# The finished fp16 rows reach x1 through 32x32 block transposes on VectorE and four plain transfers per pair of units, in place of two DMA transposes

## Chip, cores and metric

One core of a Trainium2 chip. The metric is the device time of one execution in microseconds; three runs of the kernel before are given with their median. A profile of one further execution shows what each engine did.

## What is computed

Four batches of 12,800 tokens with 128 channels. 49 agents per batch gather the values (softmax over the keys), and hand them out again to the queries (softmax over the agents). On the result x stand a gated causal convolution of five taps and an output projection:

```python
a2k = sm(agents, k)                 # 49 x 12800
agent_v = a2k @ v                   # 49 x 128
x = sm(q, agents) @ agent_v         # 12800 x 128
gate = sigmoid(sum_k conv_w[k] * x shifted by 4 - k)
out = (gate * (x @ w_val)) @ w_out
```

## The kernel before

x itself is never formed. agent_v, the conv weights and w_val are folded per batch into one set of matrices (`fold_weights`), so gate and value are matmuls of these with the query softmax weights. To keep precision with fp16 matmuls, each weight w stands as a high part and a low part in fp16. 49 high, 49 low and a second copy of 49 high make 147 rows; 128 of them stand in the tile `x1` (one row per partition, tokens along the free side), the 19 left over are put five times, once per tap shift, into the tile `x2` (95 rows).

The work runs in units of 1280 tokens, 10 units per batch (40 in all, g = 0 to 39); two units make a pair that shares one `x1` tile of 2560 tokens (ring of 4) and one `x2` tile (ring of 3). For each unit:

- `key_scores` and `agent_values`: scores of the keys (8 matmuls into the PSUM tile `sc`), copied to `ks`; later exp, VectorE's 32x32 transposes into `eT`, and 10 groups of matmuls into `av`.
- `queries`: scores into `sc`, VectorE transposes them to token-major `sT`; maximum, subtraction (POOL), exp (ACT), sum (VectorE), scaling (POOL) make the weights w in `qw`; then w is split into `pt`, 128 fp16 columns per token: ACT copies the high part, POOL writes the second copy (`again`) and the low part.
- `transposes`: brings `pt` to the row layout of `x1`. Units 0 to 3 go through TensorE and PSUM (`on_pe`). Units 4 to 39 go by one DMA transpose each (L845). `shifts` then sends the 19 rows into `x2` by two transfers per pair (L894), and `halo` copies four columns for the next pair.

Then chunks of 512 tokens, 25 per batch: `gates` (five matmuls of `x1`, L932, one of `x2`, L936, then tanh on ACT), `values` (L959, L963, then h = (th + 1) * val on VectorE, L972, and its split into `hh` on ACT and `hl` on POOL), `project` (L1004 to L1006, copied out by ACT and stored). The PSUM tiles gate, val, out and av exist once, `sc` twice.

The order: a long string lists PE's steps (k, v, q, t, g, a, o with batch and unit, or chunk). `Plan` records every instruction group with an estimated duration, its needs and its engine; PE's groups stand exactly in the order of the string, while the other engines and the DMA queue (all issued from SP, in order) are ordered by a list scheduler from those estimates. A transfer issued from SP that waits holds up those behind it. Loads go round a ring of 11 slots `ld`.

Of the kernel before, what the change touches and what calls it, by code (L numbers as in the profile page):

```python
# [10 lines left out]
F16 = mybir.dt.float16  # L11
# [6 lines left out]
P = 128  # L18
# [23 lines left out]
NPT = 4  # L42
# [148 lines left out]
def tile_agent_attention_gated_conv(  # L191
# [42 lines left out]
    pts = ring(NPT, [P, NBLK, P], F16, "pt")  # L234
# [198 lines left out]
    def key_max(b):  # L433
# [16 lines left out]
        def spread():  # L450
            nc.vector.tensor_reduce(
                out=mrow, in_=p1[0:2, 0:P].rearrange("j (g a) -> j a g", g=G),
                axis=AX.X, op=ALU.max,
            )
            nc.vector.tensor_copy(
                out=mrep, in_=mrow.unsqueeze(1).to_broadcast([2, G, BLK])
            )

        add("dve", 0.5, spread, [at1], ["mrep"])
# [61 lines left out]
    gs = const.tile([P, TAPS, A], F32, name="gs")  # L521
    rs = const.tile([P, 2], F32, name="rs")
# [4 lines left out]
    def fold_weights(b):  # L527
# [58 lines left out]
        ghi = wst[:, 0:TAPS, 0:A]  # L586
        vhi = wst[:, TAPS, 0:A]

        def thirds(x, first, end):
            return x[..., first:end:3]  # L590

        def lows(low, full, hi, less):


            for out, first, end in zip(low, (2, 0, 1, LAST), (A, LAST, A, A)):
                less(out, thirds(full, first, end), thirds(hi, first, end))

        def rest(out, full, s, hi):
            dve.scalar_tensor_tensor(
                out=out, in0=full, scalar=rs[:, s : s + 1], in1=hi,  # L600
                op0=ALU.mult, op1=ALU.subtract,
            )

        def val_weights():
# [9 lines left out]
            dve.tensor_scalar_mul(vhi, pv[:, 0:A], rs[:, 1:2])  # L614
            low = (
                wst[:, TAPS, 2 * A : 2 * A + THIRDS], wst[:, TAPS, 2 * A + THIRDS :],
                x2v[:, HALO, 0:THIRDS], x2v[:, HALO, THIRDS:],
            )
            lows(low, pv[:, 0:A], vhi, lambda out, full, hi: rest(out, full, 1, hi))

        gate_lows = (
            wst[:, 0:TAPS, 2 * A : 2 * A + THIRDS], wst[:, 0:TAPS, 2 * A + THIRDS :],
            x2g[:, :, 0:THIRDS], x2g[:, :, THIRDS:],
        )

        def gate_weights():
            dve.tensor_scalar_mul(ghi, gw, rs[:, 0:1])
# [6 lines left out]
        def gate_rest_pool():  # L634
# [10 lines left out]
        if b == 0:  # L645
            add("pool", 0.47, gate_scaled, ["gw", "rsg"], ["gs"])
            add("act", 0.4, lambda: nc.scalar.copy(out=ghi, in_=gs), ["gs"], [(*w_, "g")])
            add("pool", 1.27, gate_rest_pool, ["gs", (*w_, "g")], [(*w_, "r")])
        else:
            add("dve", 0.47, gate_weights, ["gw", "rsg"], [(*w_, "g")])  # L650
        add("dve", 1.58, val_weights, [at_v], [(*w_, "v"), "mxv"])
        add(
            "act", 0.4,
            lambda: nc.scalar.copy(out=wst[:, 0:TAPS, A : 2 * A], in_=ghi),
            [(*w_, "g")], [(*w_, "d")],
        )
# [10 lines left out]
        def transposes():  # L667
# [6 lines left out]
            "pe", 0.6, transposes, [(*w_, n) for n in "derv"] + [(*w_, "g")], [at_w],  # L674
# [68 lines left out]
    def queries(b, u):  # L743
# [7 lines left out]
        pt = pts[g % NPT]  # L751
# [27 lines left out]
        def weigh():  # L779
# [8 lines left out]
        p_ = ("pt", g % NPT)  # L788
        add(
            "act", 0.6, lambda: nc.scalar.copy(out=pt[:, :, A : 2 * A], in_=w),  # L790
            [("qw", g % NPT)], [(*p_, 0)],
        )

        def again():
            for o, end, first, last in ((2 * A, 2 * A + THIRDS, 2, A), (2 * A + THIRDS, P, 0, LAST)):
                nc.gpsimd.tensor_scalar(
                    out=pt[:, :, o:end], in0=w[:, :, first:last:3],
                    scalar1=1.0, scalar2=0.0, op0=ALU.mult, op1=ALU.add,
                )

        add("pool", 0.76, again, [("qw", g % NPT)], [(*p_, 2)])
        add(
            "pool", 1.09,
            lambda: nc.gpsimd.tensor_tensor(  # L804
                out=pt[:, :, 0:A], in0=w, in1=pt[:, :, A : 2 * A], op=ALU.subtract
            ),
            [("qw", g % NPT), (*p_, 0)], [(*p_, 1)],
        )
    def on_pe(b, u):
# [7 lines left out]
    def row_keys(s, halves):  # L817


        i = s % NX  # L820
        return [(x, i, h) for h in halves for x in ("x1", "x1b")] + [("x1h", i)] * (0 in halves)

    def halo(s):
# [4 lines left out]
        else:  # L828
# [3 lines left out]
            read = [(x, (s - 1) % NX, 1) for x in ("x1", "x1b")]  # L832
# [372 lines left out]
```

## Time and profile before

| what | value |
|---|---|
| median of three runs | 417.81 us (415.74, 417.81, 419.00) |
| the profiled execution | 415.52 us, of which span 413.4 us |
| granted TensorE clock, mean | 0.991 |
| busy PE / DVE / ACT / POOL | 395.0 / 256.0 / 297.8 / 282.1 us |
| DMA moved | 127.63 MB in 75,130 packets, 50,466 of them under 512 B |

The span runs from the first to the last instruction. Busy time of PE is modelled from the matmuls' starts, and pipelined matmuls overlap, so a busy PE is not by itself a PE at its peak. PEld is the weight load, DVE VectorE, ACT ScalarE, POOL GpSimd, SP the engine that issues the DMAs.

### The profile page before, as it was taken

Reading aid. Unit: us, or ns where it says so; the run is one execution under the profiler, and the core shown is the slowest. Engines: PE = TensorE matmul, PEld = TensorE weight load, DVE = VectorE, ACT = ScalarE, POOL = GpSimd, SP = SyncE. Lnnn points to the kernel's source line nnn. Section 1 sums busy time; section 2 is a strip of 40 time slices with the busy share of each in tenths; the row PEclk is TensorE's granted clock in tenths of the full one; section 3 lists DMA queues with packets and bytes.
Section 4 is the critical chain, followed back from the end, with each engine's and each line's share of the span. In section 5 each row is a group of like instructions: output and inputs, shape, how many; then the busy total and the mean of one; then the engine's idle time right before and its main releaser. Section 6 shows DMA issues by size and latency. Waiting matters only on the chain.

```text
span 413.4 us, 10115 instructions
## 1 busy us (share of the span) xinstructions
PE 395.0 (96%) x3905; PEld 197.1 (48%) x3905; DVE 256.0 (62%) x489; ACT 297.8 (72%) x519; POOL 282.1 (68%) x381
## 2 busy tenths in 40 slices
PE   4859999999999999999999999999999999999996
PEld 2348544445555434445446544445465544444443
DVE  3758688854835857566745687576664697643231
ACT  2564568597884777869885677689886676888875
POOL 1003679766878698656788775896578789998752
PEclk9969999999999999999999999999999999999999
DMA  8999999999999999999999999999999999999933
GB/s 323 420 416 411 366 360 357 284 358 252 350 320 267 336 269 317 337 306 330 346 356 296 298 347 311 340 303 342 310 348 313 261 302 291 223 251 232 216 144 138
DMA packets 75130, 127.63 MB, mean 309 GB/s; under 512 B 50466, under 2 KB 50850, under 8 KB 75084
## 3 DMA queue, kind: packets, MB, share of 16 engines
q1 hardware_dynamic: 74940, 126.87, 99.9%
q8 instruction: 30, 0.49, 0.5%
q10 hardware_dynamic: 144, 0.13, 0.2%
q14 instruction: 16, 0.13, 0.1%
HBM read 79.25 MB, written 26.21 MB: 255 GB/s over the span
## 4 chain that ended last, share of the span: by engine, by line
PE 85%; DMA 7%; ACT 3%; DVE 3%; POOL 1%; issue 1%; SPq 0%; DVEq 0%; ACTq 0%
PE gate L932 25%; PE sc L390 17%; PE av L494 11%; PE out L1004 5%; PE val L959 5%; PE gate L936 5%; PE val L963 5%; PE out L1005 5%; PE out L1006 5%; DMA ld<-kT 4%; DMA x<-x 2%; ACT e L485 1%; ACT th L945 1%; PE sc L859 1%; DVE h L972 0%
## 5 line engine op out<-in xcount | busy, mean ns | idle before, releaser
L985 POOL TENSOR_TENSOR hl<-h,hh 128x512 f16<-128x512 f32 x99 | 114.6, 1160 | 57.4 <-ACT hh L980 55.0
L932 PE MATMUL gate<-x,stat 128*128 128x512 f16 (+1 forms) x500 | 124.3, 378 | 0.6 <-ACT e L485 0.4
L972 DVE SCALAR_TENSOR_TENSOR h<-th,val 128x512 f32<-128x512 f32 x100 | 68.1, 681 | 81.6 <-PE out L1005 27.8
L390 PE MATMUL sc<-ld,ag_sb 128*32 128x320 f32 x1280 | 97.1, 442 | 7.5 <-DMA ld<-kT 6.3
L1025 ACT ACTIVATE ob<-out,oscale 128x512 f32<-128x512 f32 x98 | 67.2, 686 | 23.4 <-PE out L1006 23.3
L945 ACT ACTIVATE th<-gate,unscale 128x512 f32<-128x512 f32 x100 | 68.5, 685 | 21.3 <-PE gate L936 19.2
L932 PEld LDWEIGHTS <-stat 128*128 128x128 f16 x505 | 47.7, 97 | 60.6 <-issue 5.5
L980 ACT CAST hh<-h 128x512 f16<-128x512 f32 x99 | 60.7, 613 | 14.4 <-DVE h L972 13.8
L762 POOL TENSOR_TENSOR qw<-sT,qmx 128x490 f32<-128x490 f32 x40 | 40.5, 1018 | 43.8 <-DVE qmx L757 41.3
L390 PEld LDWEIGHTS sc<-ld,ag_sb 128*32 128x32 f32 x1280 | 37.9, 111 | 54.9 <-issue 17.4
L494 PE MATMUL av<-ld,eT 128*32 128x129 f32 (+1 forms) x1400 | 50.5, 277 | 2.2 <-DVE eT L400 2.2
L494 PEld LDWEIGHTS av<-ld,eT 128*32 128x32 f32 (+1 forms) x1400 | 45.6, 115 | 10.3 <-issue 3.4
L416 ACT COPY ks<-sc 128x640 f32<-128x640 f32 x40 | 27.6, 693 | 27.3 <-PE sc L390 25.1
L400 DVE STREAM_TRANSPOSE sT<-sc 128x640 f32<-128x640 f32 x40 | 33.5, 842 | 19.9 <-PE sc L390 19.1
L400 DVE STREAM_TRANSPOSE eT<-e 128x640 f32<-128x640 f32 x40 | 33.5, 839 | 19.1 <-ACT e L485 11.2
L804 POOL TENSOR_TENSOR pt<-qw,pt 128x490 f16<-128x490 f32 x40 | 43.9, 1104 | 1.9 <-ACT pt L790 1.8
L485 ACT ACTIVATE e<-ks,kbias 128x320 f32<-128x320 f32 x80 | 39.4, 554 | 7.4 <-DVE eT L400 4.6
L783 POOL TENSOR_TENSOR qw<-qw,qr 128x490 f32<-128x490 f32 x40 | 40.3, 1009 | 3.3
L936 PE MATMUL gate<-x,stat 95*128 95x512 f16 x100 | 38.0, 380 | 0.8 <-DMA x<-x 0.8
L959 PE MATMUL val<-x,stat 128*128 128x512 f16 x100 | 38.0, 380 | 0.1
L425 DVE TENSOR_REDUCE kmx<-ks 128x2 f32<-128x640 f32 x39 | 31.5, 811 | 10.5 <-ACT ks L416 10.5
L963 PE MATMUL val<-x,stat 95*128 95x512 f16 x100 | 38.0, 380 | 0.0
(133 smaller groups left out, 407.7 us busy)
## 6 DMA issues: line engine op xcount, KB each, us to landing
ld<-kT SPq DMA_DIRECT2D x40, 640.0 KB, 7.0
ld<-qT SPq DMA_DIRECT2D x40, 640.0 KB, 9.1
ld<-vP SPq DMA_DIRECT2D x39, 645.0 KB, 6.5
outT<-ob SPq DMA_DIRECT2D x48, 512.0 KB, 7.2
x<-x SPq DMA_DIRECT2D x18, 400.0 KB, 5.2
x<-x SPq DMA_DIRECT2D x18, 75.0 KB
x<-x SPq DMA_DIRECT2D x4, 200.0 KB
outT<-ob SPq DMA_DIRECT2D x3, 256.0 KB
```

The lines of the kernel that those rows point to most:

```text
L390: nc.tensor.matmul(out=out[g * BLK : (g + 1) * BLK, j, 0:GT], lhsT=ag_sb[:, b, j * BLK : (j + 1) * BLK], rhs=src[:, g * GT : (g + 1) * GT] ...
L400: nc.vector.transpose(out=out.rearrange("p n (j i) -> p j n i", j=2), in_=in_.rearrange("p j (n i) -> p j n i", i=BLK),)
L494: nc.tensor.matmul(out=av[o + j : o + j + cols, 0 : C + 1], lhsT=et[:, n, j : j + cols], rhs=vt[:, n, :], start=(u == 0 and n < 2), stop=( ...
L932: nc.tensor.matmul(out=pg, lhsT=stat[:, k, :], rhs=x1[:, c : c + w], start=(k == 0), stop=False,)
L936: nc.tensor.matmul(out=pg, lhsT=stat[0 : TAPS * X2R, TAPS + 1, :], rhs=x2[0 : TAPS * X2R, o2 : o2 + w], start=False, stop=True,)
L945: lambda: nc.scalar.activation(out=th, in_=pg, func=AF.Tanh, scale=unscale[:, 0:1]),
L959: nc.tensor.matmul(out=pv, lhsT=stat[:, TAPS, :], rhs=x1s[(b * NCH + n0 // CH) // 5 % NX][:, PAD + o2 : PAD + o2 + w], start=True, stop=False,
L963: nc.tensor.matmul(out=pv, lhsT=stat[0 : TAPS * X2R, TAPS + 2, :], rhs=x2[0 : TAPS * X2R, o2 : o2 + w], start=False, stop=True,)
L972: lambda: nc.vector.scalar_tensor_tensor(out=h, in0=th, scalar=1.0, in1=pv, op0=ALU.add, op1=ALU.mult),
L980: "act", 0.18 + 0.43 * scale, lambda: nc.scalar.copy(out=hh, in_=h),
L985: lambda: nc.gpsimd.tensor_tensor(out=hl, in0=h, in1=hh, op=ALU.subtract),
L1025: lambda: nc.scalar.activation(out=ob[:, o : o + w], in_=po, func=AF.Copy, scale=oscale if w == CH else 1.0),
```

## The change

The 128 columns of `pt` get another order: column 4r + k, with k = 0 and 1 the high and low part of agent r, and k = 2 and 3 those of agent 17 + r (15 of the columns of k = 3, whose agents stood twice, hold the second copy of a high part). VectorE then transposes each unit in blocks of 32 tokens by 32 columns (fixed k) into a tile `pr`, whose strip of 32 partitions holds the rows of 320 tokens of each unit of the pair (the queries are laid out for that on the host). When both units of a pair are through, four plain transfers, one per strip, spread 32 partitions x 4 rows over the 128 rows of `x1`, 640 tokens each. The rings change: `qw` from 4 to 3, `pt` from 4 to 2, `pr` has 2 pairs. The second copy's split (`again`) is one POOL instruction in place of two; the fold builds its matrices in the new row order, with some small operations moved from VectorE to ACT and POOL; the order string is another.

```diff
-NPT = 4
+NPT = 3
+NPR = 2
...
-    pts = ring(NPT, [P, NBLK, P], F16, "pt")
+    pts = ring(2, [P, NBLK, P], F16, "pt")
+    prs = ring(NPR, [P, G, 2 * GT], F16, "pr")
...
+        add(
+            "act", 0.25,
+            lambda: nc.scalar.copy(out=mrep, in_=mrow.unsqueeze(1).to_broadcast([2, G, BLK])),
+            ["mrow"], ["mrep"],
+        )
...
         add(
-            "act", 0.6, lambda: nc.scalar.copy(out=pt[:, :, A : 2 * A], in_=w),
+            "act", 0.72, lambda: nc.scalar.copy(out=pt4[:, :, 0::2], in_=two()),
             [("qw", g % NPT)], [(*p_, 0)],
         )
-
-        def again():
-            for o, end, first, last in ((2 * A, 2 * A + THIRDS, 2, A), (2 * A + THIRDS, P, 0, LAST)):
-                nc.gpsimd.tensor_scalar(
-                    out=pt[:, :, o:end], in0=w[:, :, first:last:3],
-                    scalar1=1.0, scalar2=0.0, op0=ALU.mult, op1=ALU.add,
-                )
-
-        add("pool", 0.76, again, [("qw", g % NPT)], [(*p_, 2)])
         add(
-            "pool", 1.09,
+            "pool", 1.4,
             lambda: nc.gpsimd.tensor_tensor(
-                out=pt[:, :, 0:A], in0=w, in1=pt[:, :, A : 2 * A], op=ALU.subtract
+                out=pt4[:, :, 1::2], in0=two(), in1=pt4[:, :, 0::2], op=ALU.subtract
             ),
             [("qw", g % NPT), (*p_, 0)], [(*p_, 1)],
         )
+        add(
+            "pool", 0.25,
+            lambda: nc.gpsimd.tensor_scalar(
+                out=pt4[:, :, 3, 0:DUP], in0=w[:, :, A - DUP :],
+                scalar1=1.0, scalar2=0.0, op0=ALU.mult, op1=ALU.add,
+            ),
+            [("qw", g % NPT), (*p_, 1)], [(*p_, 1)],
+        )
+        if on_pe(b, u):
+            return
+        h, i_ = g % 2, g // 2 % NPR
+        pr = prs[i_][:, :, h * GT : (h + 1) * GT]
+        add(
+            "dve", 1.37,
+            lambda: nc.vector.transpose(
+                out=pr.rearrange("p k (n i) -> p n k i", i=BLK),
+                in_=pt4,
+            ),
+            [(*p_, n) for n in range(2)], [("pr", i_, k, h) for k in range(2)],
+        )
...
+    def strips(g):
...
+        i, s = g // 2 % NPR, g // 2 % NX
+        pr, x1 = prs[i], x1s[s]
+        for strip in range(G):
+            src = pr[strip * BLK : (strip + 1) * BLK]
+            dst = x1[:, PAD + strip * 2 * GT : PAD + (strip + 1) * 2 * GT]
+            add(
+                "dma", 0.95,
+                lambda src=src, dst=dst: nc.sync.dma_start(out=dst, in_=src),
+                [("pr", i, k, h) for k in range(2) for h in range(2)], [(ROWS[strip % 2], s, strip // 2)], 0.68,
+            )
...
         if not on_pe(b, u):
-            dst = unit_rows(g)
-            add(
-                "dma", 1.4,
-                lambda: nc.sync.dma_start_transpose(
-                    out=dst.rearrange("p (n i) -> p n i", i=P),
-                    in_=pt.rearrange("p n r -> p (n r)"),
-                ),
-                [(*p_, n) for n in range(3)], [("x1", g // 2 % NX, g % 2)], 2.4,
-            )
-            shifts(b, u)
+            if g % 2:
+                strips(g)
+                shifts(b, u)
             return
...
-        "k0.4 k0.1 k0.7 k0.9 k0.5 k0.0 k0.8 k0.6 k0.2 k0.3 m0 m0 v0.0 v0.1 v0.2 q0.0 v0.3 v0.4 "
+        "k0.7 k0.5 k0.1 k0.3 k0.6 k0.8 k0.2 k0.4 k0.0 k0.9 m0 m0 q0.1 q0.0 v0.0 v0.1 v0.2 v0.3 "
...
-        "q3.4 q3.5 g73 f3 o71 a73 g74 a74 o72 t3.4 f3 g75 o73 q3.7 q3.8 q3.6 a75 g76 a76 f3 o74 "
+        "a73 f3 o72 g74 o71 f3 a74 g75 f3 q3.6 a75 o73 g76 o74 t3.2 a76 g77 o75 a77 g78 t3.5 a78 "
+        "o76 g79 a79 q3.7 g80 o79 g81 o77 a80 q3.9 g82 o78 a81 q3.8 o80 g83 a82 o81 g84 a83 t3.7 "
```

Three places show how the change moves instructions. First PE, from the maximum of the keys of batch 0 on (`val<-ident,m` and `gate<-ident,mrep`), before. `sc<-ld` is a score group (key or query, by the load slot), `av<-ld` a group of agent values:

```order
L446 MATMUL val<-ident,m_77 2x128
L463 MATMUL gate<-ident,mrep 128x2
L494 MATMUL av<-ld_71,eT_82 64x129 x10
L494 MATMUL av<-ld_61,eT_83 64x129 x10
L494 MATMUL av<-ld_62,eT_84 64x129 x10
L390 MATMUL sc_135<-ld_63,ag_sb 32x320 x8
L494 MATMUL av<-ld_64,eT_82 64x129 x10
L494 MATMUL av<-ld_65,eT_83 64x129 x10
L494 MATMUL av<-ld_66,eT_84 64x129 x10
L494 MATMUL av<-ld_67,eT_82 64x129 x10
L390 MATMUL sc_134<-ld_68,ag_sb 32x320 x8
L494 MATMUL av<-ld_69,eT_83 64x129 x10
```

and now (L391 is the score line there, L498 that of the agent values):

```order
L447 MATMUL val<-ident,m_77 2x128
L467 MATMUL gate<-ident,mrep 128x2
L391 MATMUL sc_134<-ld_71,ag_sb 32x320 x8
L391 MATMUL sc_133<-ld_61,ag_sb 32x320 x8
L498 MATMUL av<-ld_62,eT_82 64x129 x10
L498 MATMUL av<-ld_63,eT_83 64x129 x10
L498 MATMUL av<-ld_64,eT_84 64x129 x10
L498 MATMUL av<-ld_65,eT_82 64x129 x10
L498 MATMUL av<-ld_66,eT_83 64x129 x10
L391 MATMUL sc_134<-ld_67,ag_sb 32x320 x8
L498 MATMUL av<-ld_68,eT_84 64x129 x10
L498 MATMUL av<-ld_69,eT_82 64x129 x10
```

The two first query scores stand ahead of all agent values now, and further score groups (two of keys of batch 1 and the third query) between them.

Second the SP queue where the rows of the first pair that goes by DMA (units 4 and 5) are sent to `x1` (`x_2`) and on to `x2` (`x_107`, now `x_106`), before:

```order
L845 DMA_TRANSPOSE x_2_103<-pt_97 128x10x128
L383 DMA ld_67<-vP 128x1290
L845 DMA_TRANSPOSE x_2_103<-pt_98 128x10x128
L383 DMA ld_68<-vP 128x1290
L383 DMA ld_69<-vP 128x1290
L383 DMA ld_70<-qT 128x1280
L894 DMA x_107<-x_2_103 80x1x2560
L894 DMA x_107<-x_2_103 15x1x2560
```

and now:

```order
L876 DMA x_2_102<-pr_98 128x1x640 x4
L384 DMA ld_70<-vP 128x1290
L384 DMA ld_71<-qT 128x1280
L384 DMA ld_61<-vP 128x1290
L928 DMA x_106<-x_2_102 80x1x2560
L928 DMA x_106<-x_2_102 15x1x2560
```

The two transposes, each behind its own unit, became one block of four transfers behind both.

Third VectorE in batch 0 behind the scores of a query (`sT`, `qmx`), around the h of three chunks, before:

```order
L400 STREAM_TRANSPOSE eT_83<-e_81 128x2x10x32
L400 STREAM_TRANSPOSE sT_85<-sc_134 128x2x10x32
L972 SCALAR_TENSOR_TENSOR h_113<-th_110,val 128x512
L757 TENSOR_REDUCE qmx_87<-sT_85 128x10
L972 SCALAR_TENSOR_TENSOR h_111<-th_108,val 128x512
```

and now:

```order
L760 TENSOR_REDUCE qmx_88<-sT_86 128x10
L1006 SCALAR_TENSOR_TENSOR h_112<-th_109,val 128x512
L823 STREAM_TRANSPOSE pr_98<-pt_96 128x10x4x32
L823 STREAM_TRANSPOSE pr_98<-pt_97 128x10x4x32
L1006 SCALAR_TENSOR_TENSOR h_110<-th_107,val 128x512
L401 STREAM_TRANSPOSE eT_82<-e_81 128x2x10x32
```

Both units' new transposes (L823) stand one behind the other ahead of the h of a chunk, which waits in VectorE's queue until they are done.

More of the change, by code (lines that the diff above doesn't have):

```diff
@@ L585, in fold_weights, with highs, lows, two @@
         x2v = wst[:, TAPS + 2, 0 : TAPS * X2R].rearrange("p (r k) -> p k r", k=TAPS)
[L586 to L598, printed above, removed]
+        def highs(x, full, copy):
+            x = x.rearrange("p t (r k) -> p t r k", k=G)
+            for out, agents in ((x[:, :, :, 0:2], full[..., 0:BLK]), (x[:, :, DUP:, 2:4], full[..., BLK:])):
+                copy(out, agents.unsqueeze(3).to_broadcast([*agents.shape, 2]))
+        def lows(x, x2, full, hi, less):
+            x = x.rearrange("p t (r k) -> p t k r", k=G)
+            def two(y):
+                return bass.AP(
+                    y.tensor, y[:, :, STEP : STEP + 1].offset,
+                    [y.ap[0], y.ap[1], (STEP, 2), (1, DUP)],
+                )
+            less(x[:, :, 2:4, 0:DUP], two(full), two(hi))
+            for out, agents in (
+                (x2[..., 0:16], slice(0, 16)), (x2[..., 16::2], slice(BLK, BLK + 2)),
+                (x2[..., 17:18], slice(16, 17)),
+            ):
+                less(out, full[..., agents], hi[..., agents])
+        def rest(out, full, hi):
             dve.scalar_tensor_tensor(
-                out=out, in0=full, scalar=rs[:, s : s + 1], in1=hi,
+                out=out, in0=full, scalar=rs[:, 1:2], in1=hi,
                 op0=ALU.mult, op1=ALU.subtract,
@@ L613, in val_weights @@
             dve.reciprocal(out=rs[:, 1:2], in_=mx[:, 1:2])
[L614 to L617, printed above, removed]
[L618 to L627 removed]
+            vhi = g16[:, TAPS:]
+            full = pv[:, 0:A].unsqueeze(1)
+            dve.tensor_scalar_mul(vhi, full, rs[:, 1:2])
+            highs(
+                wst[:, TAPS : TAPS + 1], full,
+                lambda out, agents: dve.tensor_scalar_mul(out, agents, rs[:, 1:2]),
+            )
+            lows(wst[:, TAPS : TAPS + 1], x2v[:, HALO:], full, vhi, rest)
         def gate_scaled():
@@ L673, in fold_weights @@
         add(
-            "pe", 0.6, transposes, [(*w_, n) for n in "derv"] + [(*w_, "g")], [at_w],
+            "pe", 0.6, transposes, [(*w_, n) for n in "grv"], [at_w],
             key="m",
@@ L820, in row_keys @@
         i = s % NX
-        return [(x, i, h) for h in halves for x in ("x1", "x1b")] + [("x1h", i)] * (0 in halves)
+        return [(x, i, h) for h in halves for x in ROWS] + [("x1h", i)] * (0 in halves)
     def halo(s):
@@ L862, in matmuls @@
                 )
-        add("pe", 0.65, matmuls, [("pt", g % NPT, n) for n in range(3)], [at], key="t")
+        add("pe", 0.65, matmuls, [("pr", g // 2 % NPR, g % 2, n) for n in range(2)], [at], key="t")
         add(
```

93 lines of the change are left out of this document (49 added, 44 removed), and 43 rows, old and new, of the table order.

## The prediction

> **What bounds the kernel now.** I start with the head of the page: the engines, the DMA engines' share in 40 slices of the span, and the shares of the chain that ended last.
>
> ```profile
> span 413.4 us, 10115 instructions
> PE 395.0 (96%) x3905; PEld 197.1 (48%) x3905; DVE 256.0 (62%) x489; ACT 297.8 (72%) x519; POOL 282.1 (68%) x381
> DMA  8999999999999999999999999999999999999933
> PE 85%; DMA 7%; ACT 3%; DVE 3%; POOL 1%; issue 1%; SPq 0%; DVEq 0%; ACTq 0%
> ```
>
> Two things look full, TensorE and the DMA engines, and the change works on the second. The first question is which of them is waited for. A busy PE need not run at its best, so I look at the spacing of its work in the chain in order of time, at busy time by stage, and at the waits that end on a DMA.
>
> ```profile
> 114.85 1.08 PE gate L932 x5
> ...
> 117.23 1.08 PE gate L932 x5
> ...
> 400.54 1.08 PE gate L932 x5
> ...
> 402.93 1.08 PE gate L932 x5
> ```
>
> ```profile
> 60.00:100.00 40.00, 39.43 (x401) 19.08 (x394) 28.18 (x49) 31.00 (x55) 31.30 (x42) 1.00 1.00 322
> 100.00:200.00 100.00, 99.15 (x1081) 48.49 (x1079) 64.22 (x123) 76.20 (x136) 71.65 (x95) 1.00 1.07 315
> 200.00:300.00 100.00, 99.94 (x965) 48.30 (x967) 65.32 (x121) 75.96 (x132) 75.20 (x100) 1.00 1.09 321
> 300.00:400.00 100.00, 99.97 (x832) 48.79 (x825) 55.52 (x104) 77.04 (x133) 81.17 (x105) 1.00 0.96 262
> ```
>
> ```profile
> PE sc L390 <- DMA ld<-kT: 6.3, 3, 5.7
> PE gate L936 <- DMA x<-x: 0.8, 1, 0.8
> ```
>
> A chunk of 512 columns (11 matmuls of gate, value and projection) takes 117.23 - 114.85 = 2.38 us in the middle, with the DMA share at 1.07, and 402.93 - 400.54 = 2.39 us at the end, when the loads are over. So PE runs the middle at the pace of the end. From 60 to 400 us PE is idle for 340 - 338.5 = 1.5 us in all. Of the waits of PE on a DMA, 6.3 us belong to the first loads and 0.8 us to one late transfer of tap rows. The DMA engines are full but not waited for: they fetch ahead. **PE sets the end from about 26 us on**, and the change removes no matmul and adds none. What is left to win is at the start, and what is to lose is a wait that puts a hole into a dense PE.
>
> **The change part by part. 1: the start.** The rows are PE's timeline, the chain, and stages of 2 us; behind the clock column (the first 0.50) stand the DMA share and GB/s.
>
> ```profile
> 7.13 12.54 DMA ld<-kT
> ...
> 46.93 1.01 POOL qw L783
> ```
>
> ```profile
> 23.94 0.26 PE L463 MATMUL gate<-ident,mrep 2*128 2x2 f32 x1 [0.62 <-DVE mrep L455]
> 26.44 5.43 PE L494 MATMUL av<-ld,eT 128*64 128x129 f32 x60 [2.24 <-DVE eT L400]
> ```
>
> ```profile
> 24.00:26.00 2.00, 0.20 (x1) 0.11 (x1) 0.62 (x2) 1.50 (x4) 0.00 (x0) 0.50 1.03 426
> 28.00:30.00 2.00, 2.00 (x23) 2.00 (x22) 1.16 (x2) 1.50 (x4) 0.00 (x0) 0.50 1.01 415
> 30.00:32.00 2.00, 2.00 (x34) 1.79 (x34) 0.86 (x2) 1.10 (x3) 0.00 (x0) 0.90 1.02 417
> ```
>
> The tenth key load lands at 19.7 us; a load of 640 KB takes 655,360 / 417 GB/s = 1.57 us behind it. PE then waits for the key maximum and, from 24.2 to 26.44 us, for the first eT. In the new PE order two query scores stand in that hole; their loads are numbers 11 and 12 and land by 19.7 + 2 x 1.57 = 22.8 us. The hole is 2.24 us long, and the clock stands at 0.50 there, so it takes 1.1 us of full-speed work: **-1.1 us**. The value blocks now land later: the last is load 25, where it was 22, so 19.7 + 15 x 1.57 = 43.3 us instead of 38.5. Three more score groups stand ahead of it and fill that time. The fold behind them has three score groups to hide under where it had five; for that I take nothing, with 2 us of loss as one end and 1.3 us of gain as the other (the weights of a query, which POOL worked off inside the fold, are no longer there; the 46.93 row of the chain gives 1.01 us, and a hop).
>
> The clock comes back at 30.4 us, about 4 us after PE began to be busy. The Trainium skill ("TensorE: Matmul & The Clock Gate", Part 1) says that the full clock returns after one busy window of about 3.4 us; PE would then be busy from 24.2 us and could have its clock a window earlier. The trace agrees with a half clock that outlasts the hole. By that rule up to 3.4 us of half speed go, another 1.7 us; the sum leaves it out.
>
> **2: PE's order.** Leaving the chunk matmuls for scores has a price:
>
> ```profile
> 101.76 1.21 PE sc L390 x16
> ...
> 104.97 1.08 PE sc L390 x16
> ...
> 107.15 0.32 PE val L959
> 107.47 0.22 PE val L963
> ```
>
> A score group costs 1.21 us behind chunk matmuls and 1.08 behind other 32-column work, and the first chunk matmul after it 0.32 instead of 0.22: 0.23 us for each excursion. I count the excursions in the two PE orders: 38 before, 45 now. 7 x 0.23 = **+1.6 us**, on the path.
>
> **3: VectorE.** 36 block transposes come in (units 4 to 39). Nearest row, the same operation on 640 fp32, with the rows that parts 3 and 4 use:
>
> ```profile
> L400 DVE STREAM_TRANSPOSE sT<-sc 128x640 f32<-128x640 f32 x40 | 33.5, 842 | 19.9 <-PE sc L390 19.1 <-POOL qw L762 0.8
> L804 POOL TENSOR_TENSOR pt<-qw,pt 128x490 f16<-128x490 f32 x40 | 43.9, 1104 | 1.9 <-ACT pt L790 1.8
> L790 ACT CAST pt<-qw 128x490 f16<-128x490 f32 x40 | 23.6, 599 | 7.2 <-POOL qw L783 7.2
> L416 ACT COPY ks<-sc 128x640 f32<-128x640 f32 x40 | 27.6, 693 | 27.3 <-PE sc L390 25.1 <-DVE kmx L425 1.8
> L796 POOL TENSOR_SCALAR pt<-qw 128x160 f16<-128x160 f32 x40 | 16.4, 411 | 0.8
> L796 POOL TENSOR_SCALAR pt<-qw 128x140 f16<-128x140 f32 x40 | 15.3, 382 | 0.0
> L972 DVE SCALAR_TENSOR_TENSOR h<-th,val 128x512 f32<-128x512 f32 x99 | 67.5, 682 | 79.7 <-PE out L1005 27.8 <-ACT th L945 20.5 <-PE val L963 17.8
> ```
>
> And the DMA transposes that go, with the time their issue holds SP (shortest, median, longest ns) and the first and last start:
>
> ```profile
> L845 SPq DMA_TRANSPOSE x<-pt x36: 1334/3230/8020, 72.3 to 386.0; - x36
> ```
>
> The new one has 1280 elements of 2 bytes. By bytes it costs 0.84 us, by elements 1.68, and if the step of four elements halves the reading, 3.4. I take 1.6, by elements with a fixed part that is not doubled: 36 x 1.6 = 58 us. Between 100 and 300 us VectorE is busy 65 us in 100; 36 transposes over the 314 us in which units now pass are 11.5 in 100 us, so 65 + 18 = 83. It stays beside PE. The cover is thin in one place: a transpose waits for POOL, and the h operation (L972) queued behind it on VectorE frees the one PSUM tile of val that PE's next value matmul needs. Between two value groups lie 2.38 - 0.43 = 1.95 us, and h takes 0.68, so 1.27 us are spare; a transpose of 1.6 ahead of h takes 0.3 more than that. About 15 of the 36 stand right ahead of an h: 0 to 5 us. I take 0, since most chunks also have a score or agent group (1.1 us) among them.
>
> The Trainium skill ("VectorE: DVE Perf Modes", The three transpose paths) puts a 128x128 bf16 block at 311 ns on VectorE: ten blocks would be 3.1 us and VectorE's sum 54 us higher. The trace disagrees: 842 ns for five blocks of fp32 are 168 ns each. The same section warns that a plain DMA which transposes by strides is 19 times slower than the DMA's own transpose; here the plain transfers move runs of 640 elements, and no run here shows such a price.
>
> **4: POOL and ACT.** Per unit POOL gives up 411 + 382 + 1104 = 1897 ns and gets a subtraction of 640 elements, 1104 x 640/490 = 1442, and a copy of 150, about 400: 55 ns less. ACT's copy grows from 599 to about 693: 40 x 0.09 = 4 us. In the folds small work moves from VectorE to ACT and POOL, some 3 to 6 us over the run. Both stay under 85% in every 100 us above: nothing on the path.
>
> **5: the transfers.** Per pair two DMA transposes go, four plain transfers of 160 KB come. The plain transfers of the tap rows on SP, and the DMA issues by line (the last number is the us to landing):
>
> ```profile
> L894 SPq DMA_DIRECT2D x<-x x44: 612/732/859, 45.2 to 390.1; - x44
> ```
>
> ```profile
> x<-x SPq DMA_DIRECT2D x18, 400.0 KB, 5.2
> x<-pt SPq DMA_TRANSPOSE x36, 11.7
> ```
>
> An issue of a transpose held SP for 3.2 us (median, above), two per pair 6.5; four plain ones at the 0.73 of the tap-row transfers hold it for 2.9. SP's loads stand less behind others, and the DMA engines get air. PE waited for neither, so this is worth 0, with the 0.8 us wait above as the most.
>
> **6: the way from scores to gate.** It gains a transpose (1.6 us), a longer subtraction (0.3) and the wait for both units; its transfers cost about what they did. For the last pair, from PE's timeline, SP's, and the chain:
>
> ```profile
> 367.05 1.28 PE L390 MATMUL sc<-ld,ag_sb 128*32 128x320 f32 x16
> ```
>
> ```profile
> 385.95 1.34 SPq L845 DMA_TRANSPOSE x<-pt  x1
> 389.43 1.48 SPq L894 DMA_DIRECT2D x<-x  x2
> ```
>
> ```profile
> 395.77 1.08 PE gate L932 x5
> ```
>
> From the scores' end (368.3) 17.6 us pass to the issue, 3.5 to the tap rows' issue; the first gate that reads them starts at 395.8, 6.3 us behind that. The new way is 2 us longer in compute, and its four issues plus a landing like the 5.2 above make 8 where 3.5 stood: 2 to 6 us longer. By the order strings the last pair's scores stand one gate earlier now (2.4 us), and the 17.6 us hold queueing that can shrink, so I take **0**.
>
> **Sum**, against the profiled execution (413.4 of span and 2.1 around it, 415.5): 415.5 - 1.1 + 1.6 = 416.0 us. The three runs have their median at 417.8, 2.3 above that execution; the middle of 416.0 and 417.8 + 0.5 = 418.3 is 417.2, and I say **417**: no change that can be told. About 1%, 4.2 us, is what a measurement of this kernel can tell, given runs from 415.7 to 419.0.
>
> **Rivals.** *Late rows, slower.* Place: pair 18 (units 36 and 37). By the order strings its last scores stood 14 gates ahead of gate 90 and now stand 10 ahead: 10 x 2.38 + 2 scores x 1.2 = 26.2 us. The last pair's way before took 395.8 - 368.3 = 27.5 us with some slack inside; 2 to 6 us longer it is 29 to 33, so PE would stand for 3 to 7 us: 417 + 5 = 422. It decides as soon as the way takes more than 26 us. For it: the tap rows are issued only 6 us ahead of their gate in the last pair. Against it: queueing on POOL is inside the 17.6, and other pairs have more room. Chance 0.14. *VectorE becomes the bound, slower.* If the transpose takes 3.4 us, VectorE has 65 + 39 = 104 us of work per 100: 4% over the 200 us in the middle, +8 us, 425. It decides from 3.1 us upward. Against it: 168 ns per block. Chance 0.08. *A better start, faster.* The clock a window earlier (-1.7), a fold without the foreign POOL work (-1.3), the two late waits (-1.5) and the -1.1 + 1.6 above: 415.5 - 4.0 = 411.5 to 413. Against it: all must come together, since 1.5 us is all that PE waits after 60 us. Chance 0.20.
>
> **How the numbers follow.** Forecast 0.58, from 413.6 to 421. The rivals beside it reach down to 411.5 and up to 425; with the top of the second left out the range is 411.5 to 424. Faster by over 1% 0.20, within 1% 0.58, slower by over 1% 0.22.
>
> **What would show it.** Right: chunks at 2.38 us, PE idle a few us at most from 60 to 400, transposes near 1.6 us, scores from 24.2 us on. Wrong: gate matmuls that wait for x transfers, val matmuls that wait for h, or a start that ends more than 3 us earlier or later.

## The result and the profile after

The changed kernel takes **433.0 us** (median of four runs, 431.5 to 435.4), the one before 418.4 us beside it (415.7 to 421.2): ratio **1.0345, 95% interval 1.0294 to 1.0396**. The forecast was 417, no change. It is 14.6 us slower and above the range, which ended at 424. Some executions run slower at a lower granted clock; ratios and intervals, here and below, leave those out and compare with runs of the kernel before in the same session, so a ratio need not be the quotient of two medians.

The head of the page of the changed kernel answers to the lines of before. Its profiled execution is the slowest of its four (435.4 us), that of before the fastest of its four (415.5): the two spans lie 20.2 us apart, where the medians lie 14.6.

```profile
span 433.6 us, 10127 instructions
PE 402.4 (93%) x3905; PEld 195.1 (45%) x3905; DVE 296.0 (68%) x509; ACT 336.0 (77%) x530; POOL 294.7 (68%) x356
DMA  8999998899889999799999999799997769555623
PE 48%; POOL 14%; ACT 13%; DMA 11%; DVE 6%; issue 5%; SPq 1%; DVEq 0%; ACTq 0%; POOLq 0%
```

The DMA engines got air, as the prediction expected, and it bought nothing. The chain that ended last was PE to 85% and is now PE to 48%: POOL and ACT together hold 27% of it, where they had 4%. VectorE grew by 40.0 us (256.0 to 296.0), where the prediction had 58 for the transposes, less a part of the small work that the folds give up: the transposes took 54.1, and more small work left than it had taken. ACT grew by 38.2 us, for which the prediction had 4 us and some of the "3 to 6 us" of the folds. POOL grew by 12.6 us, where it had 40 x 55 ns less and the rest of those folds. The groups by form say which instructions:

```profile
L799 ACT CAST pt<-qw 128x640 f16<-128x640 f32 x36 | 58.7, 1645 | 2.4 <-POOL qw L786 2.3
L804 POOL TENSOR_TENSOR pt<-qw,pt 128x640 f16<-128x640 f32 x36 | 59.4, 1654 | 14.5 <-ACT pt L799 14.5
L811 POOL TENSOR_SCALAR pt<-qw 128x150 f16<-128x150 f32 x36 | 19.2, 556 | 1.4
L823 DVE STREAM_TRANSPOSE pr<-pt 128x1280 f16<-128x1280 f16 x36 | 54.1, 1506 | 19.1 <-POOL pt L811 9.6 <-POOL x L856 7.1 <-POOL qr L783 2.0
```

The cast of the high parts took 599 ns for 490 elements and takes 1645 for 640: 2.7 times as long for 1.3 times the elements. The subtraction takes 1654 for 1104, the copy of 150 takes 556. VectorE's transpose, for which the prediction had 1.6 us, takes 1.51. What the cast, the subtraction and the copy have in common: they write single fp16 elements into columns 4r + k, eight bytes from one to the next.

What PE waits for between 60 and 400 us, before:

```profile
PE gate L936 <- DMA x<-x: 0.8, 1, 0.8
PE gate L932 <- ACT th L945: 0.2, 1, 0.2
```

and after:

```profile
PE gate L966 <- ACT th L979: 4.5, 7, 1.1
PE val L993 <- DVE h L1006: 2.6, 5, 0.8
PE out L1040 <- POOL hl L1019: 1.0, 2, 0.6
PE gate L970 <- DMA x<-x: 1.0, 1, 1.0
```

There is no new big wait, and the rows come in time but for 1.0 us. PE waits in many small pieces, most of all for th, the tanh of a gate chunk on ACT, which frees the only gate tile of PSUM. The longest of these pieces ends at 159.77 us. From the timelines of PE, POOL and ACT:

```profile
157.18 0.38 PE L970 MATMUL gate<-x,stat 95*128 95x512 f16 x1
...
159.77 1.24 PE L966 MATMUL gate<-x,stat 128*128 128x512 f16 x5 [1.10 <-ACT th L979]
```

```profile
155.92 1.66 POOL L804 TENSOR_TENSOR pt<-qw,pt 128x640 f16<-128x640 f32 x1 [1.76 <-ACT pt L799]
157.49 1.01 POOL L765 TENSOR_TENSOR qw<-sT,qmx 128x490 f32<-128x490 f32 x1
```

```profile
154.20 1.65 ACT L799 CAST pt<-qw 128x640 f16<-128x640 f32 x1 [1.26 <-POOL qw L786]
...
158.53 0.61 ACT L773 ACTIVATE qw<-qw 128x490 f32<-128x490 f32 x1 [1.57 <-POOL qw L765]
159.05 0.67 ACT L979 ACTIVATE th<-gate,unscale 128x512 f32<-128x512 f32 x1
```

The gate chunk is finished at 157.6. Its tanh could follow at once, but ahead of it in ACT's queue stands the exp of a later unit (L773), and that waits for POOL's subtraction of the maximum (L765), which stands behind POOL's split (L804), which had waited 1.76 us for ACT's cast (L799). Two engines, each idle for over 1.5 us in this stretch, hand the strided cast and the strided split on to a tanh that has nothing to do with either.

The waits in these lines are 9.1 us together. To see how much was lost in all, I worked it out from the starts of PE's matmuls: the time from each start to the next, less the packed spacing of that matmul (216.8 ns for 512 columns; 67.5 for one of a score group; 27.5 for one of the agent values, 55 in batch 0; 56 for the small ones). The time before the first matmul counts as lost. The work is the same in both kernels, so the three columns add up to the difference of the spans.

| lost on PE, us | up to 60 us | from 60 us on | behind the last matmul's start |
|---|---|---|---|
| before | 20.9 | 13.5 | 3.4 |
| after | 23.1 | 29.3 | 5.7 |

So 15.8 of the 20.2 us between these two executions were lost in the dense part, which the prediction had called covered. A second execution of before's program (under "The price of the step by itself") lost 22.4 and 15.6 us, so differences of 2 us in this table say little.

### The profile page after: what moved, and what is told of

Same layout as the page of the kernel before. It is cut to its first block, busy times and chain, and to the rows that moved or that the text cites. A ratio compares the mean times of both kernels' runs of the same rounds, so it can differ in the third digit from the quotient of the medians.

```text
span 433.6 us, 10127 instructions
## 1 busy us (share of the span) xinstructions
PE 402.4 (93%) x3905; PEld 195.1 (45%) x3905; DVE 296.0 (68%) x509; ACT 336.0 (77%) x530; POOL 294.7 (68%) x356
## 4 chain that ended last, share of the span: by engine, by line
PE 48%; POOL 14%; ACT 13%; DMA 11%; DVE 6%; issue 5%; SPq 1%; DVEq 0%; ACTq 0%; POOLq 0%
PE gate L966 14%; PE sc L391 9%; PE av L498 6%; DMA x<-x 6%; POOL pt L804 6%; ACT pt L799 6%; DMA ld<-kT 5%; PE out L1038 3%; PE gate L970 3%; PE out L1040 3%; PE val L993 3%; PE out L1039 3%; PE val L997 3%; POOL hl L1019 2%; DVE h L1006 2%
## 5 line engine op out<-in xcount | busy, mean ns | idle before, releaser
L391 PE MATMUL sc<-ld,ag_sb 128*32 128x320 f32 x1280 | 101.2, 450 | 10.6 <-DMA ld<-kT 9.2
L1059 ACT ACTIVATE ob<-out,oscale 128x512 f32<-128x512 f32 x98 | 67.1, 685 | 14.6 <-PE out L1040 14.2
L1014 ACT CAST hh<-h 128x512 f16<-128x512 f32 x99 | 61.4, 621 | 19.3 <-DVE h L1006 18.9
L804 POOL TENSOR_TENSOR pt<-qw,pt 128x640 f16<-128x640 f32 x36 | 59.4, 1654 | 14.5 <-ACT pt L799 14.5
L765 POOL TENSOR_TENSOR qw<-sT,qmx 128x490 f32<-128x490 f32 x40 | 40.6, 1017 | 39.8 <-DVE qmx L760 39.6
L823 DVE STREAM_TRANSPOSE pr<-pt 128x1280 f16<-128x1280 f16 x36 | 54.1, 1506 | 19.1 <-POOL pt L811 9.6
L391 PEld LDWEIGHTS sc<-ld,ag_sb 128*32 128x32 f32 x1280 | 38.2, 112 | 59.0 <-issue 24.6
L799 ACT CAST pt<-qw 128x640 f16<-128x640 f32 x36 | 58.7, 1645 | 2.4 <-POOL qw L786 2.3
L498 PE MATMUL av<-ld,eT 128*32 128x129 f32 (+1 forms) x1400 | 49.5, 274 | 0.2 <-DVE eT L401 0.2
L498 PEld LDWEIGHTS av<-ld,eT 128*32 128x32 f32 (+1 forms) x1400 | 44.0, 113 | 10.7 <-issue 3.0
```

The costliest lines, as they stand in the source:

```text
L391: nc.tensor.matmul(out=out[g * BLK : (g + 1) * BLK, j, 0:GT], lhsT=ag_sb[:, b, j * BLK : (j + 1) * BLK], rhs=src[:, g * GT : (g + 1) * GT] ...
L498: nc.tensor.matmul(out=av[o + j : o + j + cols, 0 : C + 1], lhsT=et[:, n, j : j + cols], rhs=vt[:, n, :], start=(u == 0 and n < 2), stop=( ...
L799: "act", 0.72, lambda: nc.scalar.copy(out=pt4[:, :, 0::2], in_=two()),
L804: lambda: nc.gpsimd.tensor_tensor(out=pt4[:, :, 1::2], in0=two(), in1=pt4[:, :, 0::2], op=ALU.subtract),
L823: lambda: nc.vector.transpose(out=pr.rearrange("p k (n i) -> p n k i", i=BLK), in_=pt4,),
L1014: "act", 0.18 + 0.43 * scale, lambda: nc.scalar.copy(out=hh, in_=h),
```

## Experiments

The first theory (S): the strided writes. The rivals: VectorE's transposes with h queued behind them (T); the order of the program, planned from durations too short (P); the later start and the extra excursions of PE (O). The expectations, shown word for word as they stood before each run, name theories A and B of their own.

### Contiguous runs in place of the strided columns

The columns of `pt` stand as four runs of 32 (column 32k + r); the transpose reads them from there, so `pr` and all behind it are the same. Units 0 to 3 stay strided.

```diff
-        pt4 = pt.rearrange("p n (r k) -> p n k r", k=G)
+        pt4 = (
+            pt.rearrange("p n (r k) -> p n k r", k=G) if on_pe(b, u)
+            else pt.rearrange("p n (k r) -> p n k r", r=BLK)
+        )
```

> The columns of pt of units 4 to 39 are laid out as four runs of 32 (k outside, agent inside), so that ACT's and POOL's split writes contiguous runs; VectorE's transposes read runs and write the same pr. Theory A (the split's writes at a step of four fp16 elements cost ACT and POOL the time, and PE waits for ACT's and POOL's other work behind them): the ACT cast falls from 1645 ns to about 700, the POOL subtraction from 1654 to 1150 to 1450, and the time to 415 to 420 us. Rival B (the new order of PE, the wait for both units, or the block transposes on VectorE cost it): the ops may get faster, but the time stays at 428 us or more.

Measured: 423.8 us, ratio 1.0088 (1.0047 to 1.0129). Groups and PE's waits from 60 to 400 us:

```profile
L802 ACT CAST pt<-qw 128x640 f16<-128x640 f32 x36 | 26.1, 729 | 1.1 <-POOL qw L786 1.1
L807 POOL TENSOR_TENSOR pt<-qw,pt 128x640 f16<-128x640 f32 x36 | 49.2, 1368 | 5.6 <-ACT pt L802 5.4
L814 POOL TENSOR_SCALAR pt<-qw 128x150 f16<-128x150 f32 x36 | 11.6, 327 | 1.4
L802 ACT CAST pr<-qw 128x640 f16<-128x640 f32 x4 | 6.5, 1632 | 0.4 <-POOL qw L786 0.2
```

```profile
PE gate L973 <- DMA x<-x: 2.5, 2, 1.8
PE val L996 <- DVE h L1009: 1.0, 2, 0.8
PE gate L969 <- ACT th L982: 0.6, 2, 0.3
```

Same elements, same inputs, same place in the order; only the address of each written element differs, and the cast falls from 1645 to 729 ns (the four units left strided still take 1632). The wait for th goes from 4.5 to 0.6 us. Of the 3.45%, 2.6 go with the strided write; 0.9% remain, so the time came out above the 415 to 420 us of theory A and far below the 428 of rival B.

### The same with ACT's cast issued twice

```diff
+        def twice():
+            nc.scalar.copy(out=pt4[:, :, 0::2], in_=two())
+            if not on_pe(b, u):
+                nc.scalar.copy(out=pt4[:, :, 0::2], in_=two())
```

> As e1_runs32, but ACT writes the cast of units 4 to 39 twice, so that ACT alone is held about 1.4 us per unit as in the changed kernel (1.65), while POOL's split stays fast. If ACT's time alone carries the loss: 426 to 431 us, with PE waiting for tanh, hh and out copies again. If POOL's slower subtraction and copy (0.4 us per unit) or the way to the rows carry it: within 3 us of e1_runs32.

Measured: 428.4 us, 1.0221 (1.0133 to 1.0308), ACT busy 333.5 us (336.0 in the changed kernel). Between 60 and 400 us PE waits 3.3 us for th in eight pieces. By the ratios ACT's time alone gives back half of what the contiguous runs had won (1.3 of 2.6%), though the intervals of the two runs all but touch. The rest is left for POOL's part and for both one behind the other; no run has POOL slow and ACT fast.

### The strided split alone, on the kernel before

Before's DMA transposes, rings and order string; only the split in columns 4r + k, all 40 units strided, with the fold of the changed kernel to match its rows (its small operations on ACT and POOL come along). The lines of the split:

```diff
+        pt4 = pt.rearrange("p n (r k) -> p n k r", k=G)
...
-            "act", 0.6, lambda: nc.scalar.copy(out=pt[:, :, A : 2 * A], in_=w),
+            "act", 0.72, lambda: nc.scalar.copy(out=pt4[:, :, 0::2], in_=two()),
...
-                out=pt[:, :, 0:A], in0=w, in1=pt[:, :, A : 2 * A], op=ALU.subtract
+                out=pt4[:, :, 1::2], in0=two(), in1=pt4[:, :, 0::2], op=ALU.subtract
...
```

> One part of the change alone: the new column order (4r + k) with its strided split on ACT and POOL, on the DMA transposes, rings and order string of before. Theory A (the strided split carries most of the loss): ACT cast 1.64 us, POOL 1.65 + 0.55, and 9 to 14 us over before, 428 to 434. If the loss needs the new way to the rows (block transposes and four transfers behind both units): within 4 us of before.

Measured: 443.3 us (437.1 to 447.8), 1.0503 (1.0408 to 1.0599), more than the 428 to 434 expected. Over the whole span PE waits 4.9 us for th in eleven pieces and 8.5 us for late rows:

```profile
PE gate L944 <- DMA x<-x: 8.5, 4, 3.3
PE gate L940 <- ACT th L953: 4.9, 11, 1.1
```

The split costs more by itself than the whole change, with no transpose on VectorE and no new order. Taking the strided writes out wins most of the loss back, and putting them into the old kernel brings one: together the two settle the cause of the larger part. The fold is not what costs it: it stands in the kernels with contiguous runs too, and the two of them that leave out most of the transposes come within 0.4% of before. How much of the 5% the late rows are is not separated.

### The price of the step by itself

The kernel before, with copies of 640 fp32 elements per partition put behind its end, at steps of 1, 2 and 4 elements of the output (and one that reads at a step of 4).

```diff
+    nc.scalar.copy(out=f16[:, 0:640], in_=src[:, 0:640])
+    nc.scalar.copy(out=f16[:, 0:1280:2], in_=src[:, 0:640])
+    nc.scalar.copy(out=f16[:, 0:2560:4], in_=src[:, 0:640])
+    nc.scalar.copy(out=f32[:, 0:640], in_=src[:, 0:640])
+    nc.scalar.copy(out=f32[:, 0:1280:2], in_=src[:, 0:640])
...
```

> The kernel before with twelve copies of 128x640 fp32 behind its last instruction, which change no output: on ACT, VectorE and POOL to fp16 at a step of 1, 2 and 4 elements, on ACT also to fp32 at a step of 1 and 2, and from a step of 4 to fp16 at a step of 1. If single fp16 elements at a wide step are slow to write: ACT 0.7 us at step 1, 1.6 at step 4. If it is the width of the step in bytes alone, fp32 at step 2 (8 bytes) is as slow; if the reading matters, the last ACT copy is slow. POOL 1.0 to 1.4 at step 1 and about 0.3 us more at step 4; VectorE the same at all steps or not, which no run has shown.

Lines 1165 to 1167 are ACT to fp16 at steps 1, 2, 4; 1169 is ACT to fp32 at step 2, which is 8 bytes too; 1170 is ACT reading fp32 at step 4 and writing contiguous fp16; 1173 is VectorE and 1176 POOL to fp16 at step 4.

```profile
L1167 ACT CAST x<-ks 128x640 f16<-128x640 f32 x1 | 1.6, 1607 | 0.0
L1176 POOL CAST x<-ks 128x640 f16<-128x640 f32 x1 | 1.6, 1600 | 0.1
L1170 ACT CAST x<-ks 128x640 f16<-128x640 f32 x1 | 1.3, 1302 | 0.0
L1166 ACT CAST x<-ks 128x640 f16<-128x640 f32 x1 | 0.9, 899 | 0.0
L1173 DVE CAST x<-ks 128x640 f16<-128x640 f32 x1 | 0.9, 877 | 0.0
L1169 ACT COPY ld<-ks 128x640 f32<-128x640 f32 x1 | 0.8, 758 | 0.0
L1165 ACT CAST x<-ks 128x640 f16<-128x640 f32 x1 | 0.7, 716 | 0.0
```

On ACT 716, 899 and 1607 ns; POOL agrees (717, 892, 1600); VectorE 494, 523 and 877. It is not the 8 bytes as such: fp32 at the same distance costs 758, against 782 without a step. Single fp16 elements, 8 bytes apart, cost ACT and POOL 2.2 times in a copy (POOL's subtraction in the kernel, slower to begin with, only 1.2 times: 1368 and 1654). Reading at a step has a price too (1302), but the changed kernel's cast reads runs of 32, so it doesn't pay that one. Each copy ran once. The expectation had POOL wrong: 1.0 to 1.4 us and 0.3 more.

### VectorE: twice the transposes, and a tenth of them

Both on the kernel with contiguous runs. First every block transpose is issued twice:

```diff
+        def blocks_twice():
+            for _ in range(2):
+                nc.vector.transpose(
```

> e1_runs32 with each block transpose issued twice (the second writes the same), so that VectorE has 1.5 us per unit more, 54 us in all. If VectorE's time or its queue ahead of h is what e1_runs32 still pays: 6 us or more over e1_runs32. If VectorE has room: within 3 us of it.

Measured: 461.9 us, 1.1045 (1.0985 to 1.1106). Who waits for h, over the whole span:

```profile
ACT hh L1020 <- DVE h L1012: 52.8, 48, 3.3
PE val L999 <- DVE h L1012: 15.8, 15, 2.2
```

VectorE is busy 347 of 459 us, 76%, and yet it decides: h stands behind the transposes in VectorE's queue, hh and PE's values stand behind h. The second 54 us of transposes cost some 38 us. PE's own wait for h is 15.8 us of this; the rest was not followed further. So the first 54 us are at the edge of the room that VectorE has, and the question is what they cost. The other direction:

```diff
-                out=pr.rearrange("p k (n i) -> p n k i", i=BLK),
-                in_=pt4,
+                out=pr.rearrange("p k (n i) -> p n k i", i=BLK)[:, 0:1],
+                in_=pt4[:, 0:1],
...
```

The rest of `pr` is set to zero once at the start.

> The changed kernel with pt in four contiguous runs (as in the first experiment), and VectorE's block transposes of units 4 to 39 cut from ten blocks a unit to one (the first 32 queries of each of the four lanes); the rest of pr holds zeros, so nine tenths of the transposition are left out. VectorE loses about 36 x 1.3 = 47 us of its 297. Theory A, the 0.9% that the contiguous runs still cost is h queued behind the transposes, and rows that come 1.3 us later: back to the kernel before within 0.4% (ratio 0.996 to 1.004), the waits of PE on h under 0.3 us. Theory B, it is the new order's seven excursions and the start: stays at 1.006 to 1.012.

Measured over ten runs: 419.4 us, 1.0036 (1.0004 to 1.0069), VectorE busy 257 us as before. By the ratios 0.5% of the 0.9 that were left belong to the transposes (the intervals overlap; a second pair below gives 0.8%). PE's waits from 60 to 400 us:

```profile
PE val L998 <- DVE h L1011: 1.0, 2, 0.8
PE gate L975 <- DMA x<-x: 0.2, 1, 0.2
```

The wait for h is the same 1.0 us in both, not under 0.3 as T expected. What went is the wait for late tap rows (2.5 to 0.2 us) and smaller pieces that no releaser names. The first of these is no firm sign: before itself waited 0.8 us for tap rows in one execution and 1.7 in another.

### The first four units too, and both

```diff
-        pt4 = (
-            pt.rearrange("p n (r k) -> p n k r", k=G) if on_pe(b, u)
-            else pt.rearrange("p n (k r) -> p n k r", r=BLK)
-        )
+        pt4 = pt.rearrange("p n (k r) -> p n k r", r=BLK)
```

> The changed kernel with contiguous runs in all 40 units: the four units that PE transposes write theirs in runs of 32 too, so the rows of these four units come out permuted (the value of the output differs there, no work is left out). Their casts fall from 1.63 to 0.73 us, their subtractions from 1.66 to 1.37: about 4 x 1.2 = 4.8 us of ACT and POOL at the start, on the chain there twice. Theory A (transposes): within 0.3% of the first experiment, 1.006 to 1.012. Theory B (the start pays the rest): gate 0 starts 1 to 2.5 us earlier than its 53.5, ratio 1.003 to 1.006.

Measured: 423.2 us, 1.0112 (1.0047 to 1.0177), gate 0 at 53.49 us. The four strided units at the start are worth nothing that can be told.

With a tenth of the transposes as well:

> Both at once: contiguous runs in all 40 units (rows of the first four units permuted) and a tenth of the block transposes (nine tenths left out). If strided writes, transposes and nothing else separate the changed kernel from the one before, the ratio is 0.993 to 1.000; if the new order itself costs its seven excursions (1.6 us) and a later start, 1.002 to 1.008.

Measured over ten runs: 419.5 us, 1.0031 (0.9994 to 1.0067). Against the run above it (1.0112) this is 0.8% less for the same nine tenths of the transposes. Without the strided writes and nearly without VectorE's transposes the changed kernel is level with the one before within the measurement, and not faster. By its middle the ratio lies where the expectation had put a cost of the new order (1.002 to 1.008), by its interval it reaches into the other branch, so it doesn't decide between them. PE's loss, worked out as above, follows the times:

| lost on PE, us | up to 60 us | from 60 us on | ratio to before |
|---|---|---|---|
| before | 20.9 | 13.5 | 1 |
| before, another execution | 22.4 | 15.6 | |
| after | 23.1 | 29.3 | 1.0345 |
| contiguous runs | 21.2 | 20.8 | 1.0088 |
| and a tenth of the transposes | 21.0 | 17.0 | 1.0036 |
| contiguous in all 40 units | 21.0 | 19.3 | 1.0112 |
| that, and a tenth of the transposes | 21.6 | 17.2 | 1.0031 |

### The order, three trials that tell little

The changed kernel with the planner's durations set to the measured ones; PE's order is the same, the other engines and SP are reordered.

```diff
-            "act", 0.72, lambda: nc.scalar.copy(out=pt4[:, :, 0::2], in_=two()),
+            "act", 1.64, lambda: nc.scalar.copy(out=pt4[:, :, 0::2], in_=two()),
...
-            "pool", 1.4,
+            "pool", 1.65,
...
-            "pool", 0.25,
+            "pool", 0.55,
...
-            "dve", 1.37,
+            "dve", 1.5,
```

> The changed kernel with nothing but the plan's durations set to the measured ones (cast 1.64, subtraction 1.65, copy 0.55, transpose 1.5), so that the list scheduler orders ACT, POOL, VectorE and SP for them; PE's order is the same. If most of the loss is misplanning (urgent work queued behind the long cast): 420 to 426 us. If it is the engines' capacity and the longer way to the rows: 429 us or more.

Measured: 480.0 us, 1.1434 (1.1337 to 1.1531), with `PE gate` waiting 37.5 us for tap rows in nine pieces. By the letter that is "429 us or more", but 47 us over the changed kernel with the same instructions is a worse order and not a lack of capacity, so neither branch foresaw it. With PE's order held, truer durations in the planner made a far worse order on the other queues. So P is neither shown nor ruled out: the first experiment shows what the strided writes cost in a program that was planned with shorter durations, and no run shows what they would cost in one planned for them from the string on.

The changed kernel with before's order string:

> The changed kernel with PE's order string of before. Rival B, in the form that the new order string costs the time: 418 to 423 us. Theory A: 429 us or more, since the slow split is still there.

Measured: 503.7 us, 1.1987 (1.1892 to 1.2082). The old string has q1.8 ahead of t1.5, and units 18 and 15 share a buffer of `pr`: later units overwrite it ahead of its transfers. So this kernel computes something else, and nothing follows from it.

The kernel before with the new string (each even unit's transfer step moved right ahead of its odd one's):

> The kernel before (its split, its DMA transposes, its rings) with the changed kernel's order string; the transpose of each even unit of a pair, which has no place of its own there, stands right ahead of the odd one's. If the order alone carries the 0.9% that e1_runs32 left (7 more excursions of PE at 0.23 us, and the other start): 420 to 425 us against 418 to 420 of before. If the order is innocent: within 1 us of before, and the rest lies with the wait for both units, VectorE's transposes or the transfers.

Measured: 433.5 us, 1.0369 (1.0311 to 1.0426), outside both branches; from 60 to 400 us one wait of 3.7 us for tap rows, and 5.1 us of waits of PE's output matmuls for POOL and ACT. A string that suits the new way doesn't suit the old one; what the new one costs in its own kernel can't be had by this exchange. The last experiment, without strided writes and with few transposes, bounds it better: -0.1 to 0.7%.

## Why the prediction was wrong, point by point

**The step that failed is part 4, the sizing of POOL and ACT.** The forecast of no change hung on it. It priced the new split by the count of its elements and ignored where they are written. ACT's cast: 693 estimated, 1645 measured. POOL's subtraction: 1442, and 1654. The copy: 400, and 556. It is the layout and not the count that was mis-sized: in contiguous runs the same three take 729, 1368 and 327 ns, within 5 to 18% of the estimates. The prediction did think of the step of four elements, but for the reader (the transpose, "if the step of four elements halves the reading"), not for the writers; its diff shows both in `pt4[:, :, 0::2]`.

**"Nothing on the path" was the second half of that step.** It argued from shares under 85% in every 100 us. After, ACT is at 82 to 84 in each:

```profile
100.00:200.00 100.00, 96.92 (x974) 46.31 (x976) 73.37 (x125) 82.94 (x132) 74.94 (x92) 1.00 0.94 321
200.00:300.00 100.00, 98.07 (x991) 47.77 (x984) 71.80 (x121) 82.14 (x129) 74.22 (x87) 1.00 0.94 313
300.00:400.00 100.00, 95.45 (x889) 45.78 (x887) 72.94 (x119) 84.17 (x132) 83.94 (x100) 1.00 0.75 245
```

That is still under 85, and PE is idle for 1.9 to 4.6 us of each 100, where it was 0.0 to 0.9. The piece at 159.77 shows how: with one gate tile, what counts is how late one instruction may come. Part 3 had worked that out for h; part 4 did it for no instruction.

**Part 1, the start: the gain was not seen.** It had -1.1 us, with +2 and -1.3 as ends for the fold. The two query scores do stand in the hole, and gate 0 starts later and not earlier: 51.96 us before, 55.54 after, 53.2 to 54.3 in the kernels with contiguous runs. Some of the 55.54 is this one execution, in which the last key scores of batch 0 had their load late and started at 21.84 us. Where they started by 20.1 us, gate 0 came at 51.96 before and at 53.2 to 53.6 in the new order; where they started after 21.3, at 53.46 in another execution of before and at 54.03 and 55.54 in the new order. So, like for like, the new order brings it 0.6 to 2.1 us later. PE's loss up to 60 us doesn't show the 1.1 us either: with the loads on time it is 21.2 and 21.0 in the new order (the first two kernels with contiguous runs in the table) and 20.9 before.

The clock is not the reason. In the changed kernel's profile it came back when it had before, at 30.6 us against 30.4 (the granted clock is the third number from the end):

```profile
28.00:30.00 2.00, 2.00 (x16) 0.40 (x8) 1.63 (x2) 2.00 (x5) 0.00 (x0) 0.50 1.02 415
30.00:32.00 2.00, 2.00 (x34) 1.96 (x32) 1.11 (x2) 0.85 (x2) 0.00 (x0) 0.85 1.02 421
```

With contiguous runs, the same order of PE, it was back at 27.0 us, and with a tenth of the transposes it never fell. With contiguous runs:

```profile
24.00:26.00 2.00, 2.00 (x20) 0.79 (x16) 1.06 (x2) 1.99 (x5) 0.00 (x0) 0.50 1.00 413
26.00:28.00 2.00, 2.00 (x26) 0.98 (x20) 1.82 (x3) 2.00 (x5) 0.00 (x0) 0.75 1.02 418
28.00:30.00 2.00, 2.00 (x40) 2.00 (x38) 1.31 (x3) 0.94 (x3) 0.00 (x0) 1.00 1.02 418
```

PE was busy from 23.46 us on there and had its full clock 3.4 us earlier than before, after 3.5 us of work, as the rule of the Trainium skill ("TensorE: Matmul & The Clock Gate", Part 1) would have it; this trace agrees. The 1.7 us that the prediction had estimated by that rule did not come out at gate 0 even so, because in this stretch a faster PE meets the loads. With the full clock throughout (a tenth of the transposes) it waits for them ahead of nearly every group:

```profile
35.15 1.32 PE L500 MATMUL av<-ld,eT 128*64 128x129 f32 x20 [0.28 <-DMA ld<-vP]
36.94 1.32 PE L500 MATMUL av<-ld,eT 128*64 128x129 f32 x20 [0.47 <-DMA ld<-vP]
40.12 1.32 PE L500 MATMUL av<-ld,eT 128*64 128x129 f32 x20 [0.40 <-DMA ld<-vP]
```

The last agent values are done at about 46 us there, and at 42.3 before; from its first matmul to gate 0 the fold then takes 6.8 us, and 9.3 before. The prediction had worked out the later loads, and took the time ahead of them as filled.

**Part 2, the excursions: +1.6 us, not isolated.** The kernel with contiguous runs and few transposes loses 17.0 us after 60 us, and before 13.5 and 15.6 in two executions. That would fit; it holds other things too, and its ratio can't tell 1.6 us from nothing. In the traces PE goes from chunk matmuls to scores or agent values 34 times before and 40 times after, 6 more by this count where the prediction had 7.

**Part 3, VectorE: the size right, the cover thin.** 1.51 us per transpose against 1.6, and 72 to 73 us busy in 100 against 83, in part because the folds' small work left VectorE. The Trainium skill's 311 ns for a 128x128 block ("VectorE: DVE Perf Modes", The three transpose paths) is not what the trace shows here: 1506 ns for ten blocks are 151 each. Part 3 took 0 between 0 and 5 us; leaving out nine tenths gave 0.5 to 0.8%, 2 to 3.5 us, inside that range, though the wait for h by itself did not change (1.0 us with and without). That the cover is thin is shown by the doubled transposes (+38 us).

**Part 5, the transfers: right.** Per pair two issues of 3.2 us became four of 0.60, the DMA share went from 1.07 to 0.94 between 100 and 200 us, and nothing came of it. Part 6, the way from scores to gate: PE waits 1.0 us for late tap rows after 60 us in the changed kernel, and 2.5 in the one with contiguous runs, where before had 0.8 (1.7 in another execution); 0 was at most 1.7 us too little.

Of the rivals, *late rows* had the right sign by luck: its time was 422, and the wait that it named, 3 to 7 us at pair 18, did not come (the one wait for tap rows is 1.0 us). *VectorE becomes the bound* did not come true at 1.5 us a transpose. No rival had ACT and POOL, because part 4 had put their price near nothing without a bound on the other side.

## What to carry to other kernels

Price an added or changed instruction by its access pattern as well as by its count: when a change interleaves fp16 columns, look at every engine that *writes* them, and ask for a layout in which the writers keep contiguous runs. Here it cost nothing: the transpose took the same from either layout (1496 and 1506 ns). An engine that is busy 75 to 85% was not free here, where single PSUM tiles tie PE to it: compare the longest instruction in its queue with the slack of the one that PE waits for. And where most of the chain was PE, taking load off full DMA engines was worth nothing; even with the strided writes gone and nine tenths of the transposes left out it was 1.0036, no gain.

## What the runs showed of the hardware

- Writing 640 fp16 elements per partition from fp32 takes ACT 716 ns contiguous, 899 at a step of two elements and 1607 at four; POOL 717, 892 and 1600; VectorE 494, 523 and 877. fp32 elements at a distance of 8 bytes cost ACT nothing (758, and 782 without a step).
- Reading fp32 at a step of four elements (16 bytes) takes ACT 1302 ns, with contiguous fp16 output, where contiguous reading takes 716.
- VectorE's block transpose of fp16 took the same with its input at a step of four elements (1506 ns for 1280 elements) and in contiguous runs (1496).
- The stretch of half clock at the start differed from profile to profile with the same order of PE: none with a tenth of the transposes, 3.4 us with contiguous runs, 6.8 in the changed kernel, 10.2 with contiguous runs in all units and a tenth of the transposes. One profile doesn't show what an order does to the clock.
